# More weight chunks converted during the first two tiles, and 48 unread products, in an attention and two-expert-layer kernel

## The chip, the core and the metric

One core of a Trainium2 chip runs the whole program. The engines are TensorE (PE, with its weight loads PEld), VectorE (DVE), ScalarE (ACT), GpSimd (POOL) and SyncE (SP), which issues most of the DMAs. The metric is the time of one execution in microseconds of the device; less is better.

## The reference, cut to what matters

```python
scores = scale * q @ k.T                     # 4 batches, 8 heads, 576 positions, head 64
scores = where(0 <= rel < 128, scores - slope[h] * |rel|, -1e9)
attn   = softmax(scores); x = (attn @ v)     # -> 2304 tokens x 512
h = x @ w_in;  r = max(h, 0);  g = s * (r * r) + b;  x = g @ w_out     # 512 -> 2048 -> 512
# top-1 of 8 experts by cosine similarity, gate = its softmax weight
out[token] = gate * (max(x @ w1[e], 0) @ w2[e])                        # 512 -> 1024 -> 512
```

All inputs are float32. The router takes an argmax, so the layers ahead of it are computed to more than one rounding of the matmul's format: each operand is split into a high part and the remainder, and three products (high x high, high x remainder, remainder x high) are added up.

## The kernel before

**Stages.** Attention works on 18 tiles of 128 tokens with 8 heads each. One head of one tile is a unit, and a call of `tick` starts a unit and advances those under way: scores on PE (`stage_A`, L241 for the first four tiles, L244 and L245 after), bias and row minimum on DVE (`stage_B`, L253), the exponential on ACT (`stage_N`, L261), a transpose on PE (`stage_C`, L277), its copy on ACT (`stage_C2`, L282), the product with v on PE (`stage_D`, L300 or L303). In the first four tiles four heads are then normalised together on DVE into xs (L311 to L313), turned on PE (`stage_T`, L329) and split into XH on ACT (L336) and XL on DVE (L337).

The gated layer works on 9 blocks of 256 tokens, in 16 steps of 128 hidden columns each. A step is `L1` (12 matmuls of 128x256, L350), the gate `G` (ACT L360 relu, DVE L362, ACT L363 gives GH, DVE L365 gives GL) and `L2` (6 matmuls of 128x512, L373, that take GH and GL). The expert layer comes last and isn't touched.

**Conversion of the weights.** `w_in` and `w_out` come as 32 chunks of 128x512 numbers of eight bytes, alternating between the two. A chunk is loaded by SP into one of three buffers (512 KB), and `conv_ops` makes it into a high and a low part in six instructions: ACT `mag` (L175), DVE `a`, `b`, `d` (L178, L181, L184), then in `e` ACT L192 (WIH or WOH) and DVE L193 (WIL or WOL). `conv` is a queue of these pieces in order, each chunk's interleaved with the next one's. `pt` takes pieces from it: each call adds `rate[0]` to an account and takes a piece for each whole one. A tick of the first four tiles calls `pt` seven times. Where a product needs a chunk that is not converted yet, `need` takes pieces until it is.

**Order of the work.** `warm` puts matmuls of zeros (L746) on PE, into bank 3. After 4 ticks the order written in the program is not the order on the engines: a scheduler places the instructions of each engine by what they depend on, up to the place where the program goes back to manual order (block 0's end, ahead of block 2). In the program's order the first half of block 0 (8 steps, with two ticks each, tiles 2 and 3) follows the first two tiles, then the first half of block 1 (8 steps, ticks of tile 4 from the fifth on), then the second halves of both blocks in turn, then block 2 and on. `hbk` are the two banks that take `L1`'s result: block 0 uses `hbk[0]`, block 1 `hbk[1]` in their first halves.

```python
def first(b, j):          # needs chunk 2j; 12 matmuls into hbk[b]
def second(b, j):         # for j > 0: needs chunk 2j - 1; L2 of the step before
rate[0] = 0.4             # from the second tick on
rate[0] = 0.65            # from the first half of block 0 on
```

Of the kernel before, what the change touches and what calls it, by code (L numbers as in the profile page):

```python
# [17 lines left out]
P = 128  # L18
# [4 lines left out]
BLK = 256  # L23
# [18 lines left out]
def moe_attention_kernel(ctx, tc, qT, kT, vN, w_in, w_out, sc_s, sc_b, bneg, tri, bmix,  # L42
                         emb, tau, w1, w2, upper, basec, descc, rcc, tokc, out):
    nc = tc.nc
# [48 lines left out]
    WIH, WIL = ([w[j // 2][:, j % 2, :] for j in range(2 * len(w))] for w in WI2)  # L93
# [140 lines left out]
    def stage_A(u, S):  # L234
        t, h, order, sl, bc, n = geom(u)
        pr, odd = divmod(h, 2)
        hb = slice(64, 128) if odd else slice(0, 64)
        o = S[:, 0:n]
        if t < NRAW:
            for i, k in enumerate(order):  # L240
                nc.tensor.matmul(S[:, i * P:(i + 1) * P], lhsT=raws[1][t][hb, pr, :], rhs=raws[0][k][hb, pr, :], start=True, stop=True)  # L241
            return
        Q, K, L = (sp.QO, sp.KO, sp.LO) if odd else (sp.QE, sp.KE, sp.LE)
        nc.tensor.matmul(o, lhsT=Q[:, pr, :], rhs=K[:, pr, sl, :], start=True, stop=False)  # L244
        nc.tensor.matmul(o, lhsT=Q[:, pr, :], rhs=L[:, pr, sl, :], start=False, stop=True)  # L245

    def stage_B(u, S):
        t, h, order, sl, bc, n = geom(u)
        s, st = sbuf(u)[:, 0:n], st_r[u % 4]
        bi, c = (bias8[h], -0.125) if t < NRAW else (bias, 2.0 ** -(h + 1))  # L250
        if t in MIXED or t in AFTER_MIXED:
            bi, bc = bmx[t in AFTER_MIXED], slice(0, 256)
        nc.vector.tensor_tensor_reduce(s, S[:, 0:n], bi[:, bc], scale=c, scalar=3.0e38,  # L253
                                       op0=ALU.add, op1=ALU.min, accum_out=st[:, 0:1])
# [18 lines left out]
    def stage_C(u, PO):  # L273
        t, h, order, sl, bc, n = geom(u)
        p = sbuf(u) if t < NRAW else sp.p[u % 2]
        for i in range(len(order) if t < NRAW else 1):
            nc.tensor.transpose(PO[:, i * 128:(i + 1) * 128], p[:, i * 128:(i + 1) * 128], ident)  # L277

    def stage_C2(u, PO):
        t, h, order, sl, bc, n = geom(u)  # L280
        if t < NRAW:
            nc.scalar.activation(PW[u % 2][:, 0:n], PO[:, 0:n], AF.Copy)  # L282
            return
        pc, pp = (PP[u % 2][:, i] for i in range(2))
        nc.scalar.activation(pp if n > P else pc, PO[:, 0:P], AF.Copy)
        if n > P:
            nc.gpsimd.tensor_tensor(pc, pp, sp.tri, op=ALU.mult)
            nc.gpsimd.tensor_tensor(pp, pp, pc, op=ALU.subtract)
# [4 lines left out]
    def stage_D(u, PO):  # L293
        t, h, order, sl, bc, n = geom(u)
        last = len(order) - 1
        if t < NRAW:
            o = outs(u)[:, h % 4 * 64:(h % 4 + 1) * 64]
            for i, k in enumerate(order):
                v = raws[2][k].rearrange("p c f -> p (c f)")[:, h * 64:(h + 1) * 64]
                nc.tensor.matmul(o, lhsT=PW[u % 2][:, i * P:(i + 1) * P], rhs=v, start=i == 0, stop=i == last)  # L300
            return
        for i, k in enumerate(order):
            nc.tensor.matmul(PO[:, 0:P], lhsT=sp.V[k % 3][:, h // 2, :], rhs=PP[u % 2][:, t - k], start=i == 0, stop=i == last)  # L303
# [22 lines left out]
    def stage_T(u):  # L326
        g = u // 4 % 2
        for i in range(2):
            nc.tensor.transpose(bank[4 + g][:, 256 + i * P:256 + (i + 1) * P], xs_r[g][:, i * P:(i + 1) * P], ident)  # L329
# [77 lines left out]
    def run(ops):  # L407
        for f in ops:
            if callable(f):
                f()  # L410
# [173 lines left out]
    rate, due = [0.0], [0.0]  # L584

    def pt():
        todo.step()
        preps.step()
        due[0] += rate[0]
        while due[0] >= 1.0:  # L590
            due[0] -= 1.0
            conv.step()

    def plan_preps(t, h):

        if t < NRAW:
            return
        if h in (0, 1):
            preps.ops += prep_q(t, 2 + h)
            if h == 1 and t + 1 < NT:  # L600
                preps.ops.append(lambda: load_qkv(t + 1, 1))
        if t + 1 < NT:
            if h == HK:
                preps.ops += prep_k(t + 1)
                if t + 2 < NT:
                    preps.ops.append(lambda: load_qkv(t + 2, 0))
            if h == HV:
                preps.ops.append(lambda: load_qkv(t + 1, 2))
            if h in (5, 6):
                preps.ops += prep_q(t + 1, h - 5)  # L610
# [11 lines left out]
    def unit(n):  # L622

        n -= LAG if n >= NRAW * H + LAG else 0
        return n if 0 <= n < UN else None
# [6 lines left out]
    def tick(Sb, POb, mid=None, attend=True, Ob=None):  # L632
        n = nu[0] if attend else 2 * UN
        if attend:
            nu[0] += 1
        u, c, d, x = (None if NRAW * H <= i < NRAW * H + LAG else unit(i) for i in (n, n - 2, n - LAG + 1, n - LAG))
        if u is not None:
            S = Sb[u % len(Sb)]
            plan_preps(*divmod(u, H))
            stage_A(u, S)  # L640
        if d is not None:
            POd = Ob[d % len(Ob)] if Ob else POb[d % len(POb)][:, 256:512]
            stage_D(d, POd)
        if c is not None:
            POc = POb[c % len(POb)]
            stage_C(c, POc)
        turn = x is not None and x % 4 == 3 and x < NRAW * H
        if turn:
            stage_T(x)
        def B():  # L650
            if u is not None:
                stage_B(u, S)

        def X():
            if d is not None:
                stage_X(d, POd)

        def U():
            if d is not None:
                stage_X(d, POd, 0)  # L660

        def V():
            if d is not None:
                stage_X(d, POd, 1)

        def C():
            if c is not None:
                stage_C2(c, POc)

        def N():  # L670
            if u is not None:
                stage_N(u)
            if turn:
                stage_Y(x)

        def E():
            if u is not None:
                stage_N(u, 0)
            if turn:
                stage_Y(x)  # L680

        def R():
            if u is not None:
                stage_N(u, 1)

        def M():
            if mid is not None:
                mid(0)

        def G():  # L690
            if mid is not None:
                mid(fill if '[' in od else ())
            elif '[' in od:
                run(fill)

        fs = dict(E=E, R=R, U=U, V=V, B=B, X=X, C=C, N=N, M=M, G=G)
        od = OR0 if n < NRAW * H else (OR if mid is not None else OR1)
        fill = [pt if z == '.' else fs[z] for z in od[od.find('[') + 1:od.find(']')]] if '[' in od else []
        od = od[:od.find('[') + 1] + od[od.find(']') + 1:]
        for z in od:  # L700
            if z == '[':
                continue
            if z == '.':
                pt()
            else:
                fs[z]()
# [17 lines left out]
    hbk = bank[4:6]  # L724
# [13 lines left out]
    def second(b, j):  # L738
        if j > 0:
            need(2 * j - 1)  # L740
            L2(gs[b], j - 1, accs[b])

    def warm(n):

        for _ in range(n):
            nc.tensor.matmul(bank[3], lhsT=zero[:, 0:P], rhs=zero, start=True, stop=True)  # L746

    warm(9)
    with tc.manual_schedule():
        for i in range(LEAD):  # L750
            tick(*wide)
            warm(1)
            if i == 1:
                rate[0] = 0.4
    for i in range(LEAD, ticks(2)):
        tick(*wide)
        warm(1)
    rate[0] = 0.65
    for j in range(SK):
        def mid(i):  # L760
            if i == 0:
                first(0, j)
            else:
                new.append(G(0, j, hbk[0], i))

        new = []
        tick(*slim, mid)
        second(0, j)
        gs[0] = new[0]
        tick(*slim)  # L770
    second(0, SK)
    while nu[0] < ticks(4):
        tick(*slim)
    to_split()
    for j in range(SK):
        first(1, j)
        if j >= J3:
            tick(**third_b)
        for _ in range(3):
            pt()  # L780
        second(1, j)
        for _ in range(2):
            pt()
        gs[1] = G(1, j, hbk[1])
        pt()
        if j == J3 - 1:
            while preps.ops:
                preps.step()
# [312 lines left out]
```

## Time and profile before

| | |
|---|---|
| median of 3 runs | 900.65 us (898.23 to 902.5) |
| profiled execution | 904.85 us, span 903.1 us |
| PE, PEld busy | 876.2 us (97%), 762.8 us (84%) |
| DVE, ACT, POOL busy | 678.1 us (75%), 643.6 us (71%), 331.1 us (37%) |

The times are those of single executions; the profiled one is an execution of its own, whose span is measured from its first to its last instruction. A busy share is a mean over stages with different limits, and matmuls overlap in the pipeline, so that the start-to-start distance of two rows, not the duration of one, says how fast PE goes.

### The profile page before, as it was taken

The page shows a single profiled execution, that of the slowest core. Times are in us where ns is not written, and L with a number is a line of the kernel's source. Part 1 is how long each engine was busy: PE and PEld are TensorE (multiplying, and loading weights), DVE is VectorE, ACT ScalarE, POOL GpSimd, SP SyncE. Part 2 cuts the span into 40 slices and gives each one's busy share as a digit, 9 for nine tenths or more (in the row PEclk, how much of TensorE's full clock was granted, in tenths as well). Part 3 has the DMA queues.
Part 4 walks back from the last instruction along what each step waited for, and adds up shares of the span by engine and source line. Part 5 has one row for each costly group of instructions (what it writes and reads, how often), then busy time and mean ns, then how long its engine had stood idle before and what let it go on. Part 6 is the DMA issues. An engine that isn't in the chain of part 4 may idle for free. (4 is left out here: it accounts for less than half of the span.)

```text
span 903.1 us, 17172 instructions
## 1 busy us (share of the span) xinstructions
PE 876.2 (97%) x5344; PEld 762.8 (84%) x5344; DVE 678.1 (75%) x1779; ACT 643.6 (71%) x1501; POOL 331.1 (37%) x555
## 2 busy tenths in 40 slices
PE   9999788999999999999999999998999999999997
PEld 5788677989999999999999999987788888888886
DVE  4788999756666666657666755477999999999995
ACT  4776777756676767766766743565898889888885
POOL 2000357655562456555655542232321212212101
PEclk9799999999999999999999999999999999999999
DMA  7344432110021011111111000647763795755200
GB/s 266 121 136 134 164 117 79 36 36 14 26 58 60 13 34 50 37 36 26 58 37 17 32 1 2 235 128 273 256 228 129 269 346 212 259 191 211 112 21 29
DMA packets 31600, 101.32 MB, mean 112 GB/s; under 512 B 8581, under 2 KB 9222, under 8 KB 24850
## 3 DMA queue, kind: packets, MB, share of 16 engines
q1 hardware_dynamic: 26562, 89.58, 29.2%
q0 software_dynamic: 4256, 9.46, 3.0%
q8 instruction: 43, 0.70, 0.3%
q10 hardware_dynamic: 688, 1.15, 0.3%
q14 instruction: 51, 0.42, 0.1%
HBM read 133.82 MB, written 10.92 MB: 160 GB/s over the span
## 5 line engine op out<-in xcount | busy, mean ns | idle before, releaser
L350 PE MATMUL bank<-XH,WIH 128*128 128x256 f32 x576 | 172.0, 299 | 1.2 <-ACT r L360 1.1
L350 PE MATMUL bank<-XL,WIH 128*128 128x256 f32 x576 | 161.9, 281 | 0.0
L350 PE MATMUL bank<-XH,WIL 128*128 128x256 f32 x576 | 161.4, 280 | 0.0
L362 DVE SCALAR_TENSOR_TENSOR bank<-bank,s_sb,r 128x256 f32<-128x256 f32 x112 | 55.1, 492 | 106.3 <-ACT r L360 106.1
L373 PE MATMUL bank<-WOH,GH 128*128 128x512 f32 x288 | 118.4, 411 | 8.1 <-ACT GH L363 8.0
L373 PE MATMUL bank<-WOH,GL 128*128 128x512 f32 x288 | 115.1, 402 | 0.5 <-DVE GL L365 0.4
L373 PE MATMUL bank<-WOL,GH 128*128 128x512 f32 x288 | 114.2, 397 | 0.0
L350 PEld LDWEIGHTS bank<-XH,WIH 128*128 128x128 f32 x576 | 109.6, 190 | 3.9 <-ACT r L360 2.3
L350 PEld LDWEIGHTS bank<-XL,WIH 128*128 128x128 f32 x576 | 110.1, 191 | 1.5
L350 PEld LDWEIGHTS bank<-XH,WIL 128*128 128x128 f32 x576 | 109.3, 190 | 0.4
L363 ACT ACTIVATE GH<-bank,b_sb 128x256 fp32r<-128x256 f32 x112 | 53.2, 475 | 68.7 <-DVE bank L362 68.7
L261 ACT ACTIVATE s<-s,st 128x256 f32<-128x256 f32 (+1 forms) x144 | 71.2, 495 | 22.4 <-DVE st L253 20.2
L360 ACT ACTIVATE r<-bank 128x256 f32<-128x256 f32 x144 | 53.9, 374 | 37.2 <-PE bank L350 33.5
L830 PE MATMUL bank<-WIH,XH 128*128 128x512 f32 x192 | 78.1, 407 | 0.0
L271 POOL TENSOR_SCALAR p<-p,st 128x128 f32<-128x128 f32 x104 | 44.5, 428 | 89.8 <-DVE st L264 67.9
L832 PE MATMUL bank<-WIL,XH 128*128 128x512 f32 x192 | 76.1, 396 | 0.0
L831 PE MATMUL bank<-WIH,XL 128*128 128x512 f32 x192 | 75.3, 392 | 0.0
L975 POOL DMA_INDIRECT out<-x,ids x23 | 25.0, 1088 | 128.5 <-ACT XH L959 109.7
L830 PE MATMUL bank<-WOH,XH 128*128 128x512 f32 x176 | 71.2, 404 | 0.0
L832 PE MATMUL bank<-WOL,XH 128*128 128x512 f32 x176 | 69.2, 393 | 1.0 <-DVE WOL L826 1.0
L831 PE MATMUL bank<-WOH,XL 128*128 128x512 f32 x176 | 68.6, 390 | 0.0
L373 PEld LDWEIGHTS bank<-WOH,GH 128*128 128x128 f32 x288 | 54.5, 189 | 16.3 <-ACT GH L363 9.7
(190 smaller groups left out, 2369.1 us busy)
## 6 DMA issues: line engine op xcount, KB each, us to landing
W1R<-w SPq DMA_DIRECT2D x46, 1024.0 KB
W2R<-w SPq DMA_DIRECT2D x46, 1024.0 KB
x<-w_out SPq DMA_DIRECT2D x12, 512.0 KB
x<-w_in SPq DMA_DIRECT2D x11, 512.0 KB
raw<-kT SPq DMA_DIRECT2D x18, 256.0 KB
raw<-qT SPq DMA_DIRECT2D x18, 256.0 KB
x1d<-x SPq DMA_DIRECT2D x7, 512.0 KB
stage<-w_in SPq DMA_DIRECT2D x5, 512.0 KB
```

What stands on the lines that cost most here:

```text
L261: nc.scalar.activation(s, s, AF.Exp, bias=st[:, 0:1], scale=-1.0, accum_out=su)
L271: nc.gpsimd.tensor_scalar(p, p if n > P else s, st[:, 3:4], 1.0, op0=ALU.mult, op1=ALU.mult)
L350: nc.tensor.matmul(o, lhsT=w[j][:, c * P:(c + 1) * P], rhs=x[:, c, :], start=n == 0, stop=n == 11)
L360: nc.scalar.activation(r, o, AF.Relu)
L362: nc.vector.scalar_tensor_tensor(q, x, s_sb, r, op0=ALU.mult, op1=ALU.mult)
L363: nc.scalar.activation(gh, q, AF.Identity, bias=b_sb)
L373: nc.tensor.matmul(acc[k], lhsT=a[:, ts], rhs=w[j], start=(j == 0 and i == 0), stop=(j == NF - 1 and i == 2))
L830: nc.tensor.matmul(o, lhsT=lh, rhs=hi, start=first, stop=False)
L831: nc.tensor.matmul(o, lhsT=ll, rhs=hi, start=False, stop=False)
L832: nc.tensor.matmul(o, lhsT=lh, rhs=lo, start=False, stop=last)
L975: nc.gpsimd.indirect_dma_start(out=out[:, :], out_offset=bass.IndirectOffsetOnAxis(ids[:, 0:1], 0), in_=y, in_offset=None, bounds_check=NT ...
```

## The change

Two rates of the conversion queue are raised, 0.4 to 0.6 and 0.65 to 0.75, and a new helper `warm_w` puts products of weights that nobody reads on PE: 128 columns of WIH[0] against 256 columns of WIH[0], into the half bank that the other block's `L1` uses. In the first half of block 0 there are two ahead of each `second` and one behind each step's second tick, in the first half of block 1 three ahead of each `second`.

```diff
+    def warm_w(n, o):
+        for _ in range(n):
+            nc.tensor.matmul(o[:, 0:BLK], lhsT=WIH[0][:, 0:P], rhs=WIH[0][:, 0:BLK], start=True, stop=True)
+
...
             if i == 1:
-                rate[0] = 0.4
+                rate[0] = 0.6
...
-    rate[0] = 0.65
+    rate[0] = 0.75
     for j in range(SK):
...
         tick(*slim, mid)
+        warm_w(2, hbk[1])
         second(0, j)
         gs[0] = new[0]
         tick(*slim)
+        warm_w(1, hbk[1])
...
             pt()
+        warm_w(3, hbk[0])
         second(1, j)
```

What the scheduler makes of it on DVE, from the second L313 of tile 1 to its L337 (xs is the normalised output of four heads, XL the remainder of its turned copy; tmp, x and stage belong to conversions). Before:

```order
L313 TENSOR_TENSOR xs_189<-bank_84,rs_187 128x256
L193 TENSOR_TENSOR WOL_137<-tmp_156,WOH_129 128x512
L181 SCALAR_TENSOR_TENSOR tmp_158<-stage_157,tmp_158 128x512
L178 TENSOR_SCALAR tmp_155<-tmp_155 128x512
L337 TENSOR_TENSOR XL_146<-bank_83,XH_143 128x2x128
```

And now:

```order
L313 TENSOR_TENSOR xs_189<-bank_84,rs_187 128x256
L181 SCALAR_TENSOR_TENSOR tmp_155<-x_95,tmp_155 128x512
L253 ISA s_192,st_167<-bank_78,bias_180 128x256
L253 ISA st_167 128x1
L184 SCALAR_TENSOR_TENSOR tmp_155<-x_95,tmp_155 128x512
L337 TENSOR_TENSOR XL_146<-bank_83,XH_143 128x2x128
L178 TENSOR_SCALAR tmp_156<-tmp_156 128x512
L253 ISA s_165,st_168<-bank_84,bias_181 128x256
```

Between the two stand three instructions in either order (an L253 has two rows); the conversions under way here are those of chunks 7 to 9 before and of chunks 12 and 13 now (counted from 0).

On DVE at the end of the conversions, WOL_1271 and WOL_1108 are the low part of the last chunk. Before:

```order
L362 SCALAR_TENSOR_TENSOR r_150<-r_150,s_sb 128x256
L264 RECIPROCAL st_170<-st_170 128x1
L253 ISA s_165,st_167<-bank_84,bmx_161 128x256
L253 ISA st_167 128x1
L193 TENSOR_TENSOR WOL_1271<-tmp_155,WOH_135 128x512
L365 SCALAR_TENSOR_TENSOR GL_154<-r_150,b_sb,GH_152 128x256
```

And now:

```order
L362 SCALAR_TENSOR_TENSOR r_150<-r_150,s_sb 128x256
L184 SCALAR_TENSOR_TENSOR tmp_155<-x_95,tmp_155 128x512
L264 RECIPROCAL st_168<-st_168 128x1
L365 SCALAR_TENSOR_TENSOR GL_154<-r_150,b_sb,GH_152 128x256
L253 ISA s_165,st_169<-bank_84,bmx_160 128x256
L253 ISA st_169 128x1
L193 TENSOR_TENSOR WOL_1108<-tmp_155,WOH_135 128x512
```

The first of these L362 is the twentieth on DVE, that of now the fourteenth: the last chunk is done six gates earlier.

On PE at the end of the first half of block 0 (WOH_131 is the high part that its eighth `L2` reads, XH_144 is block 1's input, whose first L1 stands in the last row; xs_189 is turned by L329). Before:

```order
L329 MATMUL bank_83<-ident,xs_189 128x128 x2
L373 MATMUL bank_80<-WOH_131,GH_152 128x512
L373 MATMUL bank_80<-WOL_139,GH_152 128x512
L373 MATMUL bank_81<-WOH_131,GH_152 128x512
L373 MATMUL bank_80<-WOH_131,GL_154 128x512
L373 MATMUL bank_81<-WOL_139,GH_152 128x512
L373 MATMUL bank_81<-WOH_131,GL_154 128x512
L350 MATMUL bank_83<-XH_144,WIH_113 128x256
```

And now:

```order
L750 MATMUL bank_82<-WIH_113 128x256 x16
L373 MATMUL bank_80<-WOH_131,GH_152 128x512
L373 MATMUL bank_80<-WOL_139,GH_152 128x512
L373 MATMUL bank_81<-WOH_131,GH_152 128x512
L329 MATMUL bank_83<-ident,xs_189 128x128 x2
L373 MATMUL bank_81<-WOL_139,GH_152 128x512
L750 MATMUL bank_82<-WIH_113 128x256 x4
L373 MATMUL bank_80<-WOH_131,GL_154 128x512
L373 MATMUL bank_81<-WOH_131,GL_154 128x512
L750 MATMUL bank_83<-WIH_113 128x256
L350 MATMUL bank_83<-XH_144,WIH_113 128x256
```

The unread products (L750) of block 1's whole first half stand here, ahead of that half.

## Rows read from the trace of the kernel before

**Rows 1.** the page's first section, PE's entry among the engines

```profile
PE 876.2 (97%) x5344; PEld 762.8 (84%) x5344; DVE 678.1 (75%) x1779; ACT 643.6 (71%) x1501; POOL 331.1 (37%) x555
```

**Rows 2.** stretches: us; busy (x instructions); granted clock, DMA share, GB/s

```profile
10.00:52.00 42.00, 39.95 (x198) 29.97 (x198) 30.70 (x93) 27.43 (x84) 0.00 (x0) 0.84 0.47 154
52.00:92.00 40.00, 38.54 (x253) 33.26 (x254) 34.40 (x88) 26.94 (x71) 2.94 (x2) 0.96 0.45 149
92.00:122.00 30.00, 23.85 (x137) 19.23 (x135) 29.15 (x56) 22.78 (x50) 11.34 (x9) 0.94 0.40 135
122.00:152.00 30.00, 23.99 (x143) 19.97 (x144) 29.58 (x71) 22.25 (x59) 19.64 (x29) 0.97 0.33 111
152.00:194.00 42.00, 41.40 (x279) 37.77 (x279) 31.16 (x110) 27.46 (x87) 26.30 (x52) 0.98 0.09 26
```

**Rows 3.** timeline of PE: start, duration, instruction, count, idle before

```profile
122.97 0.51 PE L373 MATMUL bank<-WOH,GH 128*128 128x512 f32 x1 [1.35 <-ACT GH L363]
...
148.45 0.50 PE L373 MATMUL bank<-WOH,GH 128*128 128x512 f32 x1 [2.56 <-ACT GH L363]
...
194.16 0.37 PE L350 MATMUL bank<-XH,WIH 128*128 128x256 f32 x1
```

**Rows 4.** timeline of DVE: first, eighth, fourteenth gate, last converted chunk

```profile
51.77 0.48 DVE L362 SCALAR_TENSOR_TENSOR r<-r,s_sb 128x256 f32<-128x256 f32 x1
...
92.42 0.47 DVE L362 SCALAR_TENSOR_TENSOR r<-r,s_sb 128x256 f32<-128x256 f32 x1
...
121.91 0.46 DVE L362 SCALAR_TENSOR_TENSOR r<-r,s_sb 128x256 f32<-128x256 f32 x1
...
152.15 0.70 DVE L193 TENSOR_TENSOR WOL<-tmp,WOH 128x512 fp32r<-128x512 f32 x1
```

**Rows 5.** waits from 85 to 152 us: in total, times, longest

```profile
PE bank L373 <- ACT GH L363: 8.0, 5, 2.6
...
ACT GH L363 <- DVE r L362: 5.1, 5, 1.7
```

**Rows 6.** timeline of DVE: first of four conversion rows, row behind them

```profile
30.61 0.68 DVE L181 SCALAR_TENSOR_TENSOR tmp<-x,tmp 128x512 uint32<-128x512 uint32 x1
...
32.75 0.42 DVE L253 CUSTOM_DVE_ANT_0 s<-bank,bias 128x256 f32<-128x256 f32 x1
```

**Rows 7.** PE from 122.9 to 148.4 us: all, L350 alone, L373 alone

```profile
122.90:148.40 25.50, 20.56 (x129) 1.00 0.31 106
...
122.90:148.40 25.50, 9.69 (x68) 1.00 0.31 106
...
122.90:148.40 25.50, 8.84 (x30) 1.00 0.31 106
```

**Rows 8.** timeline of PE when packed: L373, first and last L350

```profile
165.50 0.39 PE L373 MATMUL bank<-WOH,GL 128*128 128x512 f32 x1
165.73 0.28 PE L350 MATMUL bank<-XH,WIH 128*128 128x256 f32 x1
...
167.00 0.28 PE L350 MATMUL bank<-XH,WIL 128*128 128x256 f32 x1
```

**Rows 9.** the stretch right behind PE's longest wait

```profile
149.80:153.50 3.70, 3.70 (x17) 3.56 (x18) 3.61 (x12) 2.91 (x10) 1.74 (x4) 0.55 0.01 4
```

**Rows 10.** DVE's waits from 10 to 52 us, the largest

```profile
DVE XL L337 <- ACT XH L336: 5.9, 3, 2.0
```

**Rows 11.** ACT's waits from 10 to 52 us, the two largest

```profile
ACT PW L282 <- PE bank L277: 7.1, 7, 1.7
ACT XH L336 <- PE bank L329: 4.5, 2, 2.3
```

**Rows 12.** PE from 52 to 92 us, L373 alone

```profile
52.00:92.00 40.00, 13.46 (x42) 0.96 0.45 149
```

**Rows 13.** timelines of POOL and DVE: two rows beside each other

```profile
94.94 1.49 POOL L210 TENSOR_TENSOR LE<-raw,KE 64x512 fp32r<-64x512 f32 x1 [3.59 <-ACT KE L208]
...
95.19 1.80 DVE L181 SCALAR_TENSOR_TENSOR tmp<-stage,tmp 128x512 uint32<-128x512 uint32 x1
```

## The prediction

> **What bounds the kernel now.** I read the engine totals first: TensorE (PE) is busy 97% of the span [rows 1]. That is a share over the whole program, and a busy PE row can be a matmul that is only waiting in the pipeline, so the second view is the table of stretches around the code that changes [rows 2]. The stretches end where the order of the work gives a mark: 52 us is the first gating step of block 0 (L362, the first row of the helper G), 92 us the eighth, 122 us the fourteenth, 152 us the last converted weight chunk, 194 us the first product of block 2 [rows 3, 4]. From there to the end each engine's order is the same in both kernels, so the whole change is worth what it does to the start of block 2.
>
> The reader is to see two regimes in [rows 2]. From 92 to 152 us VectorE (DVE) is busy 29.15 of 30 us and 29.58 of 30 us, while PE has 6 us of real gaps in each; from 152 to 194 us PE is busy 41.40 of 42 us and DVE only 31.16. So DVE binds until the conversions end, PE binds after. The waits agree: between 85 and 152 us PE's largest wait is L373 for GH, 8.0 us in 5 waits, and ACT's GH waits for DVE's r [rows 5]: the gate of a step is queued on DVE behind the conversions. Before 92 us nobody is full: DVE has 42 - 30.70 = 11.3 us idle from 10 to 52 us and 40 - 34.40 = 5.6 us from 52 to 92 us [rows 2]. This is the room into which the change puts conversions.
>
> **The change part by part.**
>
> *Conversions moved forward.* The work is not changed, only its place: 128 DVE rows (four for each of 32 chunks) in both kernels. In DVE's order 38 of them stand ahead of the first L362 before and 54 now; ahead of the eighth 78 and 100; ahead of the fourteenth 102 and 126. So 16 rows more are done before the first mark, 6 more between the first and the eighth, 2 more between the eighth and the fourteenth, and after the fourteenth 2 are left where 26 were. Price of a row: four of them, L181, L193, L184, L178, start at 30.61 and the next instruction at 32.75 us [rows 6], 2.14 us a chunk, 0.535 us a row. The moved rows are 8.6, 3.2 and 1.1 us, 12.9 us in all. ACT gets two rows a chunk as well, some 0.65 us each; it is busy 27.43 of 42 us in the first stretch [rows 2] and has the room. The loads follow at the same pace: 54 rows in 42 us are 13.5 chunks of 512 KB, about 165 GB/s on an average that was 154 GB/s with other loads in it [rows 2]; the DMA share is 0.47 there [rows 2], so I cost them at nothing, and if that cover went it would be a wait in the first stretch, where nothing but attention is late.
>
> *What comes back after the fourteenth gate.* Before, PE starts that step's L373 at 122.97 us and the packed run at 148.45 us [rows 3]: 25.5 us. In it stand 68 L350, 30 L373 and 31 small matmuls of attention [rows 7]. At full pace an L350 follows the last in 0.115 us and an L373 in 0.23 us [rows 8]; the small ones are some 0.11 us, near the L350. That is 7.8 + 6.9 + 3.4 = 18.1 us, so 7.4 us are waiting for DVE. [...] Less about 1 us for an order that packs less well than these counts, 8 us come back. What is late next is PE itself, packed as from 153.5 us on.
>
> *What the forward rows cost.* If DVE were never idle otherwise, the fourteenth gate would come 12.9 us later; if all of the 16.9 us idle took them up, not later at all. Which one depends on how full DVE can run while attention hands work around in small steps. The nearest rows: 86% from 52 to 92 us, 97 to 99% from 92 to 152 us. I take 90%, near the lower, because the long idle pieces are answers that come late, not lack of work: XL (L337) waits 5.9 us in 3 waits for ACT's XH, which itself waits for PE's turn of xs (L329) [rows 10, 11], and in the changed order two of these pairs L313, L337 still have only three DVE instructions between them. Then the first stretch is (30.7 + 8.6) / 0.9 = 43.7 us instead of 42, the second (34.4 + 3.2) / 0.9 = 41.8 instead of 40, and with 1.1 us behind it the fourteenth gate is 1.7 + 1.8 + 1.1 = 4.6 us late. At 86% it would be 8.5 us, at 98% 2.4 us early.
>
> *Unread products.* 24 in block 0's loop and 24 in block 1's, 128x256, the shape of an L350: 0.115 us each at full pace, 5.5 us, and twice that at the lower clock. 45 of the 48 stand on PE ahead of block 1's first L350 and three behind its first twelve, since nothing holds those of block 1 back: 21 come close together at the end of block 0's loop. From 52 to 92 us PE starts 253 matmuls [rows 2], 42 of them L373 [rows 12]: 253 x 0.115 + 42 x 0.115 = 33.9 us of packed work in 40, so I cost them at nothing, hidden beside DVE; if that cover is gone they cost at most 5.5 us, and the bunch alone 2.5 us. I count no gain from the clock: it was 0.96 and 0.94 in the stretches where they run [rows 2], and its slow pieces there lie beside a DVE that binds.
>
> **Sum.** 8 us back, 4.6 us paid: 3.4 us less. The profiled execution took 904.85 us (span 903.1), so 901.4 in its terms; it lay 4.2 us above the median of the runs, 900.65, and I forecast 897.3 us, 0.4% less. About 0.5%, 4.5 us, is what a measurement of this kernel can tell from no change, so this is a forecast of "within 0.5%, on the fast side".
>
> [...] A conversion row (L181) at 95.19 us takes 1.80 us, beside GpSimd's L210 from 94.94 us on, 1.49 us long [rows 13]; the row at 30.61 us takes 0.68 [rows 6], and GpSimd is idle in the first stretch [rows 2]. [...]
>
> **The rivals.**
>
> *A. The idle time takes all of it.* DVE runs as full as in [rows 2] after 92 us, 97%. For it: the conversions need nothing from attention and stand between its rows, so they can fill waits. Against it: the pairs L313, L337 named above. At 97% the two stretches take 40.5 and 38.8 us, so the fourteenth gate comes 1.6 us early and 9.6 us are gained; with the idle pieces of the first ticks left as they are, on time and 8. I put 8.6: 892 us.
>
> *B. The queue is in order, and each forward row delays the chain of attention: slower.* Place: the first two tiles, where a tick goes DVE (L253), ACT (L261), PE, ACT (L282), PE, and each step answers the one before. A conversion in front of an L253 or L313 delays the whole chain by 0.6 us, and the idle time just moves. For it: ACT's largest waits there are 7.1 us for PE's L277 and 4.5 us for L329 [rows 11]; DVE is idle 27% of the first stretch although conversions were pending. Against it: the scheduler moved attention's rows among them anew. Price: all 12.9 us, against 8 back, 4.9 us slower: 905.5 us. It decides from where DVE ends up at 86% in the first 92 us (8.5 us paid) down. [...]
>
> *C. The products are not hidden, and eat the gain.* The bunch of 21 falls where DVE's gate of step 7 lets PE go, and the others delay block 0's products. 2.5 to 4 us of 5.5 show: 900.5 us, no change. For it: PE is 38.54 of 40 us busy from 52 to 92 [rows 2]. Against it: that count includes waiting in the pipeline.
>
> **How the numbers follow.** The forecast (a gain of 0 to 4.5 us around 3.4) has 0.45, A 0.27, B 0.14, C 0.14. A lies beyond 0.5% wholly, and a tenth comes from the forecast's own spread: faster 0.37. C and the rest of the forecast: same 0.50. Most of B: slower 0.13. The range runs from A's 890 (its 892 with 2 us for the spread of the runs) to B's edge at 904.5.
>
> **What would show it.** In the changed profile the last L193 lies near 127 us instead of 152, and no L373 waits over 2 us for GH behind it. The eighth L362 comes at 94 to 97 us and the fourteenth at 125 to 128 (A: 91 and 121; B: 104 and 135). Block 2 starts near 191 us (A: 186; B: 199). DVE is busy about 90% from 10 to 95 us. The 48 products sit in PE's idle time. I am wrong if the first stretch grows by over 4 us, if PE is not packed behind the fourteenth gate, or if time changes after block 2 has started.

## The result, and the profile after

The changed kernel took 913.85 us (median of 9 runs, 906.93 to 920.66), the kernel before 901.07 us (9 runs, 897.82 to 904.25) beside it: a ratio of 1.0118, 95% interval 1.0085 to 1.015. That is slower by 1.2%, where I had forecast 897.3 us and no measurable change. The same kernel timed again (experiment 1) gave 1.0117 (1.0075 to 1.0159). Ratios are formed from the runs within 1.5% of the fastest of their kernel, so they are not the quotients of the medians: by the ratio the change costs 10.6 us, between the medians 12.8.

The profiled executions stand closer, 907.78 us (span 905.9) against 904.85 (903.1), because single times of both kernels spread over 18 us (the kernel before, over its runs beside the experiments, 891.77 to 910.02), and the execution profiled before lay high in its spread, the one after low. So the traces are read by stretches and by pairs of experiments, not by their ends. First the engine totals, then the five stretches of [rows 2], both of after:

```profile
PE 877.0 (97%) x5392; PEld 764.5 (84%) x5392; DVE 673.1 (74%) x1779; ACT 644.0 (71%) x1501; POOL 322.6 (36%) x555
```

```profile
10.00:52.00 42.00, 32.93 (x166) 23.30 (x166) 35.13 (x97) 29.18 (x80) 0.00 (x0) 0.74 0.62 202
52.00:92.00 40.00, 38.64 (x239) 32.07 (x238) 33.30 (x88) 27.55 (x71) 0.00 (x0) 0.93 0.42 137
92.00:122.00 30.00, 25.88 (x162) 22.04 (x161) 26.36 (x50) 20.46 (x45) 8.83 (x6) 0.95 0.47 150
122.00:152.00 30.00, 26.37 (x172) 22.73 (x171) 27.03 (x81) 21.86 (x64) 18.54 (x31) 1.00 0.16 43
152.00:194.00 42.00, 42.00 (x296) 38.82 (x294) 26.46 (x93) 27.20 (x85) 25.56 (x52) 1.00 0.10 32
```

PE has its 48 instructions more, and is packed in the last stretch, as forecast. But in the first stretch it starts 166 matmuls where it started 198, at a clock of 0.74 where it was 0.84: attention is further behind. The marks of [rows 3, 4] say by how much. The gates one, eight and fourteen and the last converted chunk on DVE, and the start of block 2 on PE:

```profile
56.92 0.49 DVE L362 SCALAR_TENSOR_TENSOR r<-r,s_sb 128x256 f32<-128x256 f32 x1 [1.53 <-ACT r L360]
...
100.83 0.45 DVE L362 SCALAR_TENSOR_TENSOR r<-r,s_sb 128x256 f32<-128x256 f32 x1
...
131.98 0.47 DVE L362 SCALAR_TENSOR_TENSOR r<-r,s_sb 128x256 f32<-128x256 f32 x1
...
134.87 0.69 DVE L193 TENSOR_TENSOR WOL<-tmp,WOH 128x512 fp32r<-128x512 f32 x1 [1.01 <-ACT WOH L192]
```

```profile
197.56 0.37 PE L350 MATMUL bank<-XH,WIH 128*128 128x256 f32 x1
```

The gates come 5.1, 8.4 and 10.1 us later than in [rows 4], where I expected 1.7, 3.5 and 4.6. From the fourteenth gate to block 2 it is 65.6 us for 72.3: 6.7 us come back, for 8 forecast. PE's waits at L373 from 85 to 152 us, in total, times, longest: those for GH, 8.0 us in [rows 5], are 1.9 now, and no wait exceeds 1.4 us:

```profile
PE bank L373 <- DVE GL L365: 2.6, 3, 1.4
PE bank L373 <- ACT GH L363: 1.9, 2, 1.2
```

What happened in between shows in slices of 10 us, here from 10 to 60 us of after (columns as in the stretches):

```profile
10.00:20.00 10.00, 7.95 (x32) 5.79 (x32) 7.12 (x23) 5.92 (x21) 0.00 (x0) 0.64 0.90 293
20.00:30.00 10.00, 10.00 (x65) 6.76 (x65) 6.57 (x25) 6.52 (x22) 0.00 (x0) 0.84 0.29 97
30.00:40.00 10.00, 6.20 (x42) 4.35 (x39) 9.97 (x23) 7.82 (x20) 0.00 (x0) 1.00 0.63 211
40.00:50.00 10.00, 6.78 (x27) 5.41 (x28) 9.48 (x24) 7.18 (x17) 0.00 (x0) 0.51 0.66 208
50.00:60.00 10.00, 9.95 (x50) 7.97 (x50) 8.30 (x22) 7.01 (x18) 0.00 (x0) 0.64 0.41 127
```

From 30 to 50 us DVE is full, 9.97 and 9.48 of 10 us. PE starves, 6.20 and 6.78 us. In the first of these two slices the granted clock is still 1.00, in the second it is 0.51, and when work comes back PE does it at 0.64. In the second slice an L350 follows the last in 0.215 us (four steps from 45.16 to 46.02 us, at a clock of 0.50), for 0.115 when packed [rows 8]. The clock was low once before, 0.64 from 10 to 20 us. These are the two candidates for the loss, and the experiments try to take them apart: the time of the rows on DVE, and the clock.

### The profile page after: what moved, and what is told of

The parts are those of the page before. It is cut to its first block, busy times and chain, and to the rows that moved or that the text cites. A ratio compares the mean times of both kernels' runs of the same rounds, so it can differ in the third digit from the quotient of the medians.

```text
span 905.9 us, 17276 instructions
## 1 busy us (share of the span) xinstructions
PE 877.0 (97%) x5392; PEld 764.5 (84%) x5392; DVE 673.1 (74%) x1779; ACT 644.0 (71%) x1501; POOL 322.6 (36%) x555
## 5 line engine op out<-in xcount | busy, mean ns | idle before, releaser
L350 PE MATMUL bank<-XH,WIH 128*128 128x256 f32 x576 | 171.1, 297 | 0.6 <-ACT r L360 0.6
L350 PE MATMUL bank<-XL,WIH 128*128 128x256 f32 x576 | 161.8, 281 | 0.0
L350 PE MATMUL bank<-XH,WIL 128*128 128x256 f32 x576 | 161.3, 280 | 0.0
L362 DVE SCALAR_TENSOR_TENSOR bank<-bank,s_sb,r 128x256 f32<-128x256 f32 x112 | 55.1, 492 | 106.5 <-ACT r L360 106.2
L373 PE MATMUL bank<-WOH,GH 128*128 128x512 f32 x288 | 118.3, 411 | 2.3 <-ACT GH L363 2.2
L373 PE MATMUL bank<-WOH,GL 128*128 128x512 f32 x288 | 114.5, 400 | 2.6 <-DVE GL L365 2.6
L373 PE MATMUL bank<-WOL,GH 128*128 128x512 f32 x288 | 114.1, 396 | 0.0
L350 PEld LDWEIGHTS bank<-XH,WIH 128*128 128x128 f32 x576 | 109.3, 190 | 3.3 <-ACT r L360 1.6
L350 PEld LDWEIGHTS bank<-XL,WIH 128*128 128x128 f32 x576 | 109.8, 191 | 1.7
L350 PEld LDWEIGHTS bank<-XH,WIL 128*128 128x128 f32 x576 | 109.1, 189 | 0.0
L271 POOL TENSOR_SCALAR p<-p,st 128x128 f32<-128x128 f32 x104 | 41.3, 397 | 84.5 <-DVE st L264 66.3
L373 PEld LDWEIGHTS bank<-WOH,GL 128*128 128x128 f32 x288 | 54.1, 189 | 16.2 <-DVE GL L365 5.1
```

The source lines that it names most:

```text
L271: nc.gpsimd.tensor_scalar(p, p if n > P else s, st[:, 3:4], 1.0, op0=ALU.mult, op1=ALU.mult)
L350: nc.tensor.matmul(o, lhsT=w[j][:, c * P:(c + 1) * P], rhs=x[:, c, :], start=n == 0, stop=n == 11)
L362: nc.vector.scalar_tensor_tensor(q, x, s_sb, r, op0=ALU.mult, op1=ALU.mult)
L373: nc.tensor.matmul(acc[k], lhsT=a[:, ts], rhs=w[j], start=(j == 0 and i == 0), stop=(j == NF - 1 and i == 2))
```

## The experiments

All ratios are against the kernel before, run beside each, with 95% intervals.

**1 to 4: which part.** The changed kernel again, and its parts alone. Both rates without the products (`rate[0] = 0.6`, `rate[0] = 0.75`, no `warm_w`); the products with the old rates; and the first rate alone:

```
-                rate[0] = 0.4
+                rate[0] = 0.6
```

> The changed kernel once more. Its profiled execution was 2.8 us of span longer than the one before the change, but its median is 12.8 us above. Theory 1 (the work order costs 3 us, and a second thing that differs between executions costs the rest): the single times lie again in two groups, near 907 and near 915 us, and a profile of an execution near 915 differs from that near 907 in one stretch, either ahead of block 2 (below 200 us) or in the expert part (after 600 us). Theory 2 (the order alone costs 1.2%): one group near 914, and every profile has block 2 starting 10 us later than before.

> Both rates raised, no unread products. Conversion rows on VectorE ahead of the gates are as in the changed kernel (54, 100 and 127 ahead of the first, eighth and fourteenth). Theory 1 (the conversions put forward delay attention's chain in the first two tiles): ratio to before 1.010 to 1.014, the first gate at 56 to 58 us, the fourteenth near 131. Theory 2 (the unread products cost, by 5.5 us of TensorE time and the order they force): ratio 0.996 to 1.002.

> The 48 unread products at the old rates; conversion rows ahead of the gates are as before the change (38, 78 and 102). Theory 1 (forward conversions cost): ratio 0.998 to 1.003, since the products lie in TensorE's waits. Theory 2 (products cost): ratio 1.006 to 1.012, with the eighth gate 3 to 6 us later than 92 us.

> Only the first rate, 0.4 to 0.6, no unread products: 54 conversion rows ahead of the first gate, 95 ahead of the eighth, 119 ahead of the fourteenth. Theory 1 (the chain of attention in the first two tiles is delayed by the forward rows): nearly all of the cost of the two rates, ratio 1.008 to 1.013, first gate at 56 to 58 us. Rival (the idle time of the first stretch takes these rows, and the second rate crowds block 0's loop): ratio 0.995 to 1.000, first gate at 52 to 54 us.

Measured: 909.71 us, 1.0117 (1.0075 to 1.0159); rates 915.54, 1.0167 (1.0107 to 1.0227); products 901.53, 1.0007 (0.9962 to 1.0053); first rate 915.86, 1.0159 (1.0095 to 1.0223), the kernel before 901.58. The first rate alone makes the whole loss. The products cost nothing that can be measured, and without them the new rates are no faster (1.0167 against 1.0117, with intervals that overlap). Experiment 1 fits neither of its theories: its times spread from 902.7 to 920.8 us, and in its trace block 2 starts at 193.4 us, 0.7 us before that of [rows 3].

The trace of the products alone was a surprise. DVE's order up to the first gate is that of the kernel before, and yet its first gate comes at 42.8 us, 9 us before that of [rows 4], and its span is 892.1. From 30 to 60 us, the slices of that run:

```profile
30.00:40.00 10.00, 9.26 (x52) 6.66 (x52) 8.94 (x28) 8.30 (x25) 0.00 (x0) 0.83 0.44 153
40.00:50.00 10.00, 10.00 (x73) 8.66 (x71) 9.26 (x27) 7.19 (x18) 0.00 (x0) 1.00 0.36 121
50.00:60.00 10.00, 9.93 (x67) 8.23 (x66) 7.58 (x21) 7.10 (x20) 0.00 (x0) 1.00 0.43 146
```

DVE is 8.94 and 9.26 busy there, with the old rates. The 11.3 us that DVE was idle in the first stretch of [rows 2] belonged to that execution: PE's clock was low in parts of it (0.71 and 0.61 from 30 to 50 us), and DVE waited for PE by way of ACT (5.9 us for XH, which itself waited 4.5 us for L329 [rows 10, 11]).

**5 to 7: the clock, by matmuls on zeros.** Each tick of the first two tiles ends with one unread 128x512 product of zeros, `warm(1)`. Two of them in both kernels, or none in the one before, to see whether the clock of these tiles makes the loss:

```
-            warm(1)
+            warm(2)
```

> The kernel before the change with two matmuls of zeros a tick in the first two tiles instead of one; conversions where they were. [...] Theory 2 (VectorE's queue alone sets the pace of these tiles): ratio 1.000 to 1.006, since only TensorE work is added.

> The changed kernel with two matmuls of zeros a tick in the first two tiles instead of one. [...] Theory 2 (the forward rows stand in the way on VectorE and ScalarE whatever the clock): ratio 1.008 to 1.015, first gate at 54 to 58 us even where the granted clock is high.

> The kernel before the change without the matmul of zeros behind each tick of the first two tiles (the nine at the start stay); conversions where they were. Theory 1 (the clock): slower like the changed kernel or more, ratio 1.008 to 1.020, granted clock under 0.65 from 10 to 50 us, first gate at 56 us or later. Theory 2 (VectorE's queue): ratio 0.995 to 1.000, since only TensorE work is taken away.

Measured: 900.44 us, 1.0022 (0.9981 to 1.0063); the changed kernel with two 908.79, 1.011 (1.0052 to 1.0167); none 907.37, 1.0092 (1.005 to 1.0135). Without the zero products the clock is 0.50 to 0.55 from 10 to 60 us and the kernel is 0.9% slower, with DVE's order up to the fourteenth gate unchanged: a low clock in these tiles is worth some 8 us, which is of the size of the loss. More of them don't bring the changed kernel back, but they don't hold its clock either: it is 0.68, 0.67 and 0.50 from 30 to 60 us.

**8: the second rate alone**, `rate[0] = 0.75` for 0.65.

> Only the second rate, 0.65 to 0.75; no unread products and the first two tiles as before the change. Theory 1 (the loss of the change is made in the first two tiles): ratio 0.993 to 1.001, since 6 to 10 conversion rows ahead of the gates are gained without touching them. Theory 2 (conversions ahead of attention's rows cost wherever they are put): ratio 1.003 to 1.010, with the stretch from the first to the eighth gate 3 us longer than 40.6 us.

Measured: 902.21 us, 1.0015 (0.9971 to 1.006). Its fourteenth gate has 112 conversion rows ahead for 102 and lies 5.4 us behind that of the products alone (117.3 for 111.9), and 4.5 us of it are given back by block 2 (67.7 for 72.2 us). These are ten moved rows at about their price, with most of it returned.

**9 and 10: the same, tied to the tick.** The zero products read nothing that a tick makes, and can run early. These two in each tick read its PW:

```
+    def busy(n, k):
+        for i in range(k if n >= 2 else 0):
+            nc.tensor.matmul(bank[i % 4][:, BLK:BLK + P], lhsT=ident, rhs=PW[n % 2][:, 0:P], start=True, stop=True)
...
+            busy(i, 2)
```

> The kernel before with two more unread 128x128 products in each tick of the first two tiles, which read the tick's own PW and so come with it, not early. Theory 1 (the length of the first two tiles is set by TensorE's granted clock there, and the clock falls where TensorE has too little to do between two ticks): the clock stays at 0.9 or more from 20 to 60 us, the first L362 comes at 43 to 46 us in every profile and the ratio is 0.988 to 0.995. Theory 2 (VectorE sets the pace and the clock follows): the ratio is 0.998 to 1.004, the first L362 near 50 us.

> The changed kernel with the same two products in each tick. Theory 1 (what was lost is the low clock that the forward conversions bring on by leaving TensorE without work): the clock stays at 0.9 or more from 20 to 60 us and most of the loss goes, ratio 1.003 or less. Theory 2 (the 24 forward rows cost their full time on a VectorE that has no room, 12.9 us paid and 7 us given back later): even at the high clock the first L362 comes about 10 us after that of the kernel before with such products, and the ratio stays at 1.005 to 1.012.

Measured: before 904.25 us, 1.0056 (1.0009 to 1.0102); changed 911.51, 1.0159 (1.0099 to 1.0218). Between these two medians lie 7.3 us. Their traces run at nearly one clock, and this is the pair that prices the rows. To the first, the eighth and the fourteenth gate, the kernel before:

```profile
10.00:48.90 38.90, 38.30 (x261) 31.75 (x265) 30.06 (x92) 27.35 (x80) 0.00 (x0) 1.00 0.47 165
48.90:89.00 40.10, 38.05 (x258) 32.81 (x258) 35.54 (x89) 27.33 (x71) 2.93 (x2) 1.00 0.45 150
89.00:118.30 29.30, 21.98 (x133) 17.92 (x133) 28.83 (x55) 22.78 (x50) 11.03 (x9) 1.00 0.40 133
```

and the changed one:

```profile
10.00:57.90 47.90, 42.09 (x260) 32.95 (x265) 38.39 (x107) 32.50 (x89) 0.00 (x0) 0.96 0.57 188
57.90:100.40 42.50, 40.73 (x271) 34.09 (x271) 36.91 (x94) 28.50 (x72) 2.75 (x2) 1.00 0.41 143
100.40:131.00 30.60, 24.48 (x155) 20.21 (x153) 29.48 (x58) 22.92 (x51) 12.39 (x13) 1.00 0.45 138
```

The reader is to see DVE's idle time in the first row of each: 38.90 - 30.06 = 8.8 us and 47.90 - 38.39 = 9.5 us. Busy time grew by 8.3 us, the stretch by 9.0; on balance nothing was filled. The gates are 9.0, 11.4 and 12.7 us late, for 9.1, 11.8 and 12.9 us of moved rows (17 rows more ahead of the first gate here, since 37 stand there without the change). Behind the fourteenth gate 6.8 us come back, and block 2 starts 5.9 us late, span 904.6 for 899.1. The first theory of the expectation, that the clock is all of it, is wrong.

Two things keep this from being the price of a row alone. The first slice of each trace, the kernel before and then the changed one:

```profile
10.00:20.00 10.00, 9.78 (x64) 7.68 (x65) 8.39 (x29) 7.09 (x23) 0.00 (x0) 1.00 0.83 306
```

```profile
10.00:20.00 10.00, 7.50 (x38) 5.89 (x39) 5.73 (x19) 4.70 (x16) 0.00 (x0) 0.83 0.88 289
```

The changed kernel runs at 0.83 there, and ACT, whose rows DVE's next ones need, stands still for a chunk that has not landed:

```profile
11.47 0.66 ACT L175 ACTIVATE tmp<-x 128x512 f32<-128x512 f32 x1 [2.21 <-DMA x<-w_out]
```

Such waits of ACT for loads sum up to 3.9 us from 8 to 62 us of the changed trace, and to nothing in the other. From 20 us on DVE's idle time does fall, from 7.22 to 5.25 us. So in this pair some idle time was filled, and a late load and a lower clock at the start made up for it. Without tied products these waits are 1.1 us before and 2.3 after; they are 1.1 to 2.8 in six traces with the old first rate and 0.4 to 4.2 in seven with 0.6, no clear difference. No experiment moved the loads alone, or ACT's rows alone.

**11: half of it**, `rate[0] = 0.5`.

> The kernel before with the first rate 0.5, half way between 0.4 and 0.6: 46 conversion rows stand ahead of the first L362 (38 before, 54 at 0.6), 86 ahead of the eighth and 111 ahead of the fourteenth. Theory 2 (each forward row costs its time): half of the loss, ratio 1.004 to 1.009, and the eighth L362 some 5 us later than before. Theory 1 (a clock that falls or does not): nearly none or nearly all of it, ratio under 1.003 or over 1.010.

Measured: 908.08 us, 1.0125 (1.0085 to 1.0165): more than half of the loss (the whole is 1.0159 in experiment 4, with an interval that overlaps). Its trace holds 0.50 from 20 to 30 and 0.51 from 40 to 50 us. Rows alone would have given about half; a clock that is low already here fits the rest.

**12: shorter rows.** In the changed kernel, VectorE's rows of the first 14 conversions on 352 of 512 columns, so that the rest of those weights is not converted:

```
+        H2 = 352 if c < 14 else 512
...
-            nc.vector.tensor_scalar(tu, tu, 3, None, op0=ALU.logical_shift_left)
+            tu_ = tu[:, 0:H2]
+            nc.vector.tensor_scalar(tu_, tu_, 3, None, op0=ALU.logical_shift_left)
```

> The changed kernel with VectorE's four rows of each of the first 14 conversions on 352 of their 512 columns (the rest of those weights is not converted, so the products with them are not the reference's): each row takes some 0.15 to 0.2 us less, 8 to 10 us of VectorE's time ahead of the fourteenth gate, loads and ScalarE rows as in the changed kernel. Theory 2 (VectorE's time is the price): the first L362 comes 5 to 10 us earlier than in the changed kernel and the ratio falls to 0.996 to 1.004. A third theory (the loads, ScalarE's rows or the order are the price): the ratio stays at 1.009 or more.

Measured: 906.51 us, 1.009 (1.0047 to 1.0134). The first gate comes at 44.9 us, but with only 44 conversion rows ahead of it (the scheduler placed them anew), and the lead is lost: the fourteenth comes at 126.0, with the 126 rows of the changed kernel ahead. One slice shows where:

```profile
40.00:50.00 10.00, 9.77 (x42) 8.65 (x42) 6.18 (x18) 5.54 (x14) 0.00 (x0) 0.53 0.58 199
```

DVE is 6.18 us busy, with PE at 0.53: ACT waits 3.1 us for PE's L1, and the high part that DVE's next row needs stands behind it in ACT's queue. So the second theory of that expectation, DVE's time alone, doesn't hold either: with the rows made cheaper most of the loss stayed. The clock fits this, but so does the third theory (loads, ACT's rows, the order), which this run leaves open; with the order held fixed nothing was measured.

**13 to 17: a wait near 640 us, and the other direction.** In six of the first fourteen profiles PE waits 5 to 7 us near 640 us, in none of the five with the old rates. I moved the weight row that it waits for from GpSimd to VectorE, and at first the wrong one (slot 1's, near 606 us, `and sl != 1`), and turned the first rate to 0.3:

> The kernel before, with one weight row near 640 us (the low part of slot 1's second up chunk, L826) on VectorE, where GpSimd had it behind two indirect DMAs. In six of fourteen profiles so far TensorE waits 5 to 7 us there for GpSimd's row, in the others 1 us. If those waits make the second level that the single times show at one and the same clock, the single times lie on one line against the clock and the median falls by 2 to 5 us: ratio 0.994 to 0.998. If the wait only moves to the next row, the ratio is 0.998 to 1.003.

> The changed kernel with the same row on VectorE. Theory 2 (the forward rows cost 12.7 us by the fourteenth gate and give 6.8 back, and the lower clock does the rest; the waits near 640 us are chance in both kernels): slower than the run above by 8 to 11 us, as the changed kernel is than the one before. Theory 4 (the change makes the long wait near 640 us more frequent, 5 of 8 profiles against none of 5, and so 3 to 5 us of the loss): slower than the run above by 5 us or less, ratio to the kernel before 1.002 or less.

> The kernel before with the first rate 0.3 for 0.4: 29 conversion rows stand ahead of the first L362 for 38, 68 for 78 ahead of the eighth and 92 for 102 ahead of the fourteenth. Theory 2 (a row costs its 0.53 us on VectorE wherever VectorE binds): the fourteenth gate 5 us earlier than with the old rates at a like clock, and 5 us given back behind it, ratio 0.997 to 1.003. If the room that I read in the first tiles were real, so that rows there are free, the ratio would be 1.004 to 1.007.

Measured: 903.82 us, 1.0065 (1.0022 to 1.0108), and 917.54, 1.0202 (1.0142 to 1.0262), which say nothing on the wait, since it was left in place; why slot 1's row on VectorE is slower wasn't followed up. The rate 0.3 gave 900.82, 1.0022 (0.9978 to 1.0066). Rows moved back gain nothing and cost nothing that can be measured; the interval reaches into the 0.4% to 0.7% that free rows in the first tiles would have lost, so this run doesn't decide. Its trace ran at 0.74 and 0.57 from 10 to 30 us, so its marks don't price the rows. Then slot 3's row, the one that was waited for:

```
-        eng = nc.gpsimd if i == 1 and sl <= 3 else nc.vector
+        eng = nc.gpsimd if i == 1 and sl <= 2 else nc.vector
```

> The kernel before with slot 3's row (near 640 us in the trace; the runs before this one had moved slot 1's, near 606 us, and left the wait in place) on VectorE instead of GpSimd. If the 5 to 7 us waits for that row make the second level of the single times, the times lie on one line against the clock and the ratio is 0.994 to 0.998; if the wait moves to the next row, 0.998 to 1.004.

> The changed kernel with slot 3's row on VectorE. Theory 2 (the forward rows and the clock in the first tiles are the whole loss, the long wait near 640 us is chance in both): slower than the run above by 8 to 11 us. Theory 4 (the long wait is 3 to 5 us of the loss): slower than the run above by 4 to 7 us, and ratio to the kernel before 1.006 or less.

Measured: the kernel before with it 891.55 us, 0.9941 (0.9911 to 0.9972), faster than both kernels; the changed one 913.94, 1.0178 (1.0124 to 1.0232). With the wait gone from both, the changed kernel is 22.4 us slower, not less: the loss doesn't need the wait. What the two differ in besides the rows is the clock, a median of 0.991 and of 0.970 over their timed runs. Their slices, first the kernel before from 30 to 60 us:

```profile
30.00:40.00 10.00, 9.05 (x50) 6.56 (x51) 7.58 (x25) 7.17 (x22) 0.00 (x0) 0.82 0.37 132
40.00:50.00 10.00, 10.00 (x65) 8.24 (x66) 9.73 (x28) 8.09 (x22) 0.00 (x0) 1.00 0.39 128
50.00:60.00 10.00, 9.93 (x71) 8.62 (x72) 8.39 (x24) 6.36 (x19) 0.00 (x0) 1.00 0.41 152
```

then the changed one from 10 to 60 us:

```profile
10.00:20.00 10.00, 8.02 (x28) 5.76 (x29) 5.89 (x19) 5.65 (x20) 0.00 (x0) 0.55 0.79 287
20.00:30.00 10.00, 9.78 (x38) 6.57 (x38) 5.18 (x22) 4.85 (x17) 0.00 (x0) 0.50 0.23 70
30.00:40.00 10.00, 10.00 (x49) 8.14 (x47) 5.27 (x12) 4.59 (x14) 0.00 (x0) 0.50 0.34 106
40.00:50.00 10.00, 7.02 (x30) 4.93 (x30) 9.62 (x23) 7.13 (x16) 0.00 (x0) 0.50 0.50 167
50.00:60.00 10.00, 7.37 (x28) 4.99 (x27) 9.38 (x26) 7.45 (x19) 0.00 (x0) 0.50 0.60 198
```

From 40 to 60 us DVE is full, PE has 7 of 10 us of work, and stays at 0.50; the first gate comes at 64.1 us for 43.1. But the clock was 0.55 and 0.50 from 10 to 30 us already, ahead of the slices in which DVE is full. So here the full DVE didn't start the low clock; what did isn't shown.

Up to the fourteenth gate DVE's order is the same in before, 13 and 16, and in after, 1, 14 and 17. Block 2 starts at 194.2, 186.2 and 183.4 us in the first three, and at 197.6, 193.4, 204.6 and 207.6 in the others: the old order spreads over 11 us, the new one over 14, and the profile before the change was the late one of its kind.

**The clock over all timed runs.** Of the 121 runs of the kernel before beside the experiments the median clock is 0.986, and 63 have 0.986 or more; of 21 runs of the changed kernel (experiment 1 included) the median is 0.978, and none has. The time goes with it: the 63 have a median span of 894.0 us, the 56 from 0.975 to 0.985 one of 901.9. The 16 of the changed kernel in that same band have 906.5. So at a like clock the change costs 4.6 us, about the 5.9 of experiments 9 and 10; all runs together differ by 908.3 - 897.1 = 11.2 us, and the other 6.6, a remainder, go with the lower clock. A straight line through the 121 runs gives 0.84 us for each 0.001 of clock, 6.7 us for the 0.008 between the two medians, but one through the 21 gives only 0.31. The bands are not clean: a clock is chosen here after the change has acted on it, and times near 913 us stand in the same band as times near 906. So I take this split as rough.

## Why the prediction was wrong

**The step that failed is "What the forward rows cost".** I took DVE's idle time before 92 us for room, and filled it to 90%: (30.7 + 8.6) / 0.9 instead of 42 + 8.6. In the profile after, DVE was busy 84% and 83% of the first two stretches, not 90%, and the first gate came 5.1 us late, past the 4 us that I had named as the sign of being wrong. Measured at nearly one clock (experiments 9 and 10), the idle time stayed (8.8 and 9.5 us) and the moved rows cost on balance their full time: 12.7 us at the fourteenth gate for 24 rows, 0.53 us each, not 4.6. How much of this a late load in that trace paid isn't shown. My own reason against (idle pieces are answers that come late, not lack of work) was the right one, and I priced it at a few points of a percentage. Two things misled me. The idle time came from one execution whose PE clock was 0.71 and 0.61 in parts of the stretch, and with the same order at a higher clock DVE is 29.30 of 32.80 us busy up to the first gate. And I took a fill of 86% before 92 us for a level that more work would raise; it did not rise.

**A term was missing: the clock.** I counted no gain from it, and no loss either, with 0.84 in the first stretch of [rows 2] in front of me. In all seven traces with the first rate at 0.6, full rows and no tied products (after, experiments 1, 2, 4, 6, 14, 17) PE has a slice between 30 and 60 us with only 5.5 to 7.0 of 10 us of work, DVE is busy 8.9 to 10.0 us in it, and the clock is 0.50 or 0.51 in it or in the slice behind it. In the six with the old first rate and zero products in each tick (before, experiments 3, 5, 8, 13, 16) the emptiest slice has 8.3 us, and the clock there goes to 0.50 in one and stays at 0.61 or more in the others. So forward rows go with a starving PE and a low clock, and with products tied to the tick the changed kernel's clock is 1.00 from 30 to 60 us. That the starving makes the fall is argued, not shown: in experiments 2, 4 and 17 the clock is 0.50 to 0.58 from 10 to 30 us already, with DVE busy only 4.2 to 7.2 us of 10, and experiment 5 has 0.50 from 20 to 30 us at the old rate. What the chip decides by was not measured.

**Point by point.** The gain behind the fourteenth gate was nearly right, 6.7 to 6.8 us for 8; PE is packed there and its waits for GH behind that gate, 3.9 us in two, are gone. The 8 us hold 7.4 of waiting, less 1 for packing, and 1.7 us for the stretch of [rows 9], reckoned as 2.0 us of work in 3.7; no run shows that last term by itself, and what the runs show is the 6.7 to 6.8 us in all. The long row of [rows 13], 1.80 us for 0.68, has no term of its own in the sum, and no run shows whether GpSimd's row beside it is the cause. Conversions ended 2.9 us after the fourteenth gate, as the order said, at 134.9 instead of 127 because that gate was late. The unread products cost nothing that the median shows (1.0007, though its interval reaches 1.0053); by the traces rival C falls, since from the first gate to block 2 it is 141.4 us with them (experiment 3) and 142.4, 140.4 and 140.3 without (before, 13, 16). Rival A, that the idle time takes all, falls furthest. The loads, which I had costed at nothing, show no clear cost but in one pair: ACT waits 1.1 us for them before, 2.3 after, and 0 and 3.9 in experiments 9 and 10. The second rate is neutral, which no part of the prediction had separated.

**Rival B was the mechanism.** Its price, all 12.9 us paid and 8 back, 4.9 us slower, is what the pair with tied products shows (12.7, 6.8, 5.9); I gave it 0.14. Its number, 905.5 us, was still short of the median by 8 us, most of it, by the rough split above, the clock, which B had not either. What it lives on, a VectorE that keeps to its queue, can be seen in the trace before (start, duration, idle time ahead):

```profile
46.21 0.68 DVE L181 SCALAR_TENSOR_TENSOR tmp<-stage,tmp 128x512 uint32<-128x512 uint32 x1
46.81 0.42 DVE L178 TENSOR_SCALAR tmp<-tmp 128x512 uint32<-128x512 uint32 x1
49.28 0.42 DVE L337 TENSOR_TENSOR XL<-bank,XH 128x256 fp32r<-128x256 f32 x1 [2.05 <-ACT XH L336]
49.62 0.68 DVE L184 SCALAR_TENSOR_TENSOR tmp<-stage,tmp 128x512 uint32<-128x512 uint32 x1
```

L184 needs only the chunk and the tmp of L181, which ended at 46.89 us, and yet DVE stands idle for 2.05 us until L337 has its XH, and starts L184 behind it. An idle time that on balance did not fall, 8.8 us without the moved rows and 9.5 with them, agrees with this.

The sum by these terms: 12.7 paid and 6.8 back are 5.9 us, measured; the measured loss is 10.6 to 12.8, so 5 to 7 us are left. The clock is the likeliest owner, at the 6.6 us of the split, but that figure is itself a remainder and proves nothing by fitting.

## What to carry to other kernels

Idle time of an engine that waits ahead of a row while a ready one stands behind it (2.05 us above), in a chain of short answers, was not room here (8.8 us without the moved rows, 9.5 with them): price each instruction put ahead at its full duration unless the row behind it is seen to wait. Before an idle time goes into a sum, look whether it belongs to the kernel or to one execution: here the granted clock of its stretch, 0.84, was the sign. And when work moves onto the engine that feeds TensorE, price TensorE's clock as a term of its own: in the seven traces above it was 0.50 or 0.51 in the slice in which TensorE had 5.5 to 7.0 of 10 us of work, or in the one behind it.

## What the runs showed of the hardware

**The same order, 9 us apart by the first gate.** The first 24 us tell executions apart, and the clock column doesn't show it: it says 1.00 from 10 to 20 us in both of the next two. The fifth L277 on PE, with DVE's order the same up to there, in the profile before and in that of experiment 8 (start, duration):

```profile
16.05 0.47 PE L277 MATMUL bank<-ident,s 128*128 128x128 f32 x1
```

```profile
12.59 0.33 PE L277 MATMUL bank<-ident,s 128*128 128x128 f32 x1
```

In the first execution these rows take 0.42 to 0.47 us up to 19.0 us and 0.27 at 24.0, in the second 0.33 from 7.3 us and 0.27 at 17.95. Until then DVE and ACT wait for PE, and by 30 us the second is 6.1 us ahead (L181 at 24.55 for the one at 30.61 in [rows 6]).

**A GpSimd row behind two indirect DMAs.** Near 640 us PE needs a weight row that GpSimd makes after issuing a scatter and a gather. The kernel before (start, duration), then the changed kernel in experiment 1:

```profile
638.80 1.87 POOL L975 DMA_INDIRECT out<-x,ids  x1 [0.30 <-ACT x L931]
640.97 1.72 POOL L840 DMA_INDIRECT xg<-x1d,ids  x1 [0.30 <-issue]
642.71 2.40 POOL L826 TENSOR_TENSOR WOL<-W1R,WOH 128x1024 fp32r<-128x1024 f32 x1
```

```profile
638.57 3.72 POOL L982 DMA_INDIRECT out<-x,ids  x1 [0.31 <-issue]
642.60 3.22 POOL L847 DMA_INDIRECT xg<-x1d,ids  x1 [0.30 <-issue]
645.83 2.36 POOL L833 TENSOR_TENSOR WOL<-W1R,WOH 128x1024 fp32r<-128x1024 f32 x1
```

And PE at the end of it, before and in experiment 1:

```profile
646.26 0.51 PE L832 MATMUL bank<-WOL,XH 128*128 128x512 f32 x1 [1.02 <-DVE WOL L826]
```

```profile
648.24 0.80 PE L839 MATMUL bank<-WOL,XH 128*128 128x512 f32 x1 [6.87 <-POOL WOL L833]
```

The same two issues take 3.59 us in one execution and 6.94 in the other, and PE waits 6.87 us. From block 2's start to the end it is 708 to 709 us where this wait is 1 us, 711 to 714 where it is 2.4 to 6.9, and 705 with the row on VectorE (experiments 16 and 17). What makes the issues long in one execution and short in the other stays open. A lead that was not followed: beside the long scatter of experiment 1 VectorE works through three weight rows of 128x1024 (637.94 to 641.42 us), beside the short one only through one (638.58 to 639.79).
